# A new order table for a gated-recurrence and MLP kernel on one core: engines, turns and places of some 1,070 steps

## The chip, the cores and the metric

The kernel runs on one core of a Trainium2 chip. A core has five engines with a queue each: TensorE (PE; its weight loads are listed apart as PEld), VectorE (DVE), ScalarE (ACT), GpSimd (POOL) and SyncE (SP, which here only issues DMAs). Each engine works its queue off in order and waits at semaphores for the others. The metric is the device time of one execution in microseconds (us), as the median of several runs.

## The reference

Inputs are q, k, v, a_re, a_im of shape (4, 8, 768, 48): batch, heads, sequence, head size. First a recurrence with a complex decay for each row of the state, then a layer norm and an MLP with a residual:

```python
mag = np.sqrt(a_re * a_re + a_im * a_im)
scale = np.minimum(mag, 0.999) / (mag + 1e-06)
a_re_n, a_im_n = (a_re * scale, a_im * scale)
...
for t in range(S):
    ...
    new_re = ar * S_re - ai * S_im
    new_im = ar * S_im + ai * S_re
    S_re, S_im = (new_re + kv, new_im)       # kv = outer(k_t, v_t)
    y[:, :, t] = q_t @ S_re
...
x = y with heads joined                       # (4, 768, 384)
xn = (x - mu) / np.sqrt(var + 1e-06) * g_ln
out = x + np.maximum(xn @ w_ch1, 0.0) @ w_ch2 # 384 -> 1536 -> 384
```

## The kernel before

**The tiling.** The sequence is cut into chunks of 128 steps. Two chunks are a pair P; three pairs make a batch, so there are 12 pairs (0 to 11) and 24 chunks n (2P and 2P+1). Pair 0 alone is worked on in two halves of the heads (`PARTS`), so its steps have names such as `r.0.0` and `r.0.1`.

**The steps of a pair**, as they are named in the order table:

- *Loads* on SP: `are`, `aim` (L440), `k`, `q`, `vf` (L399). The weights come by two DMAs from POOL's queue: `wl.0` (w1b, L359) and `wl.1` (w2b, L361).
- *Decay.* `ln` and `iv` on ACT (L443, L445: logarithm of a_re and its reciprocal), `r` (L289: a_im/a_re), `r2` (its square, on ACT L453 or by multiplication L289), `u` (ACT L457: log of 1 + r2), `l` and `lc` (DVE L461, L464), `dec` (PE L472: running sums), `e` and `en` (ACT L476: exponentials). `th` (ACT L480: arctangent), `ph` (PE L487, L491: running phase), `car` (the phase carried to the next pair), `sin`, `cos` (ACT L509, L520, L532), with `qt` (PE L516) or `abs` (L526, L528) between them.
- *Products.* `ke`, `qe`: k times en, q times e (two halves m of 384 elements). `ks`, `qs`: these times cosine (a = 0) and sine (a = 1), 768 elements each. All are multiplications at L289 on DVE or POOL. `dps`, `decc`: the decay at the end of the pair.
- *Chunk by chunk.* `kT`, `qT` (PE transposes, L588) with the copies `ksT`, `qsT` out of PSUM (L284 on ACT, L286 on DVE), or the same by one transposing DMA on SP (L593). `am` (PE L611: 8 products of qsT and ksT), `atm` (DVE: times a triangular mask), `gm` and `G` (the state, L635, L639), `y` (PE L661, L664), `x` (its copy), `bn` (DVE L674, L675), `xtr`, `xT` (transposed x).
- *MLP.* `mm1` (PE L715) in three groups, `relu` (ACT L726 or DVE L728), `mm2` (PE L736), `rstd` (L698 to L703), `ot` (on DVE in one step, L750; or `oa` on ACT, L741, and `ot` on POOL, L748), `st` (the store, SP L756). `wp`, `wc` fold the layer norm into w1b before the first `mm1`.

Steps with logarithm and exponential need one table set of ACT, those with arctangent and sine another: `tab.log` and `tab.trig` are the loads (L770). `warm` (L765) are matmuls without use for their result, at the start.

**What sets the order.** Nothing is scheduled by a program: `PLAN` is a table of tokens `name:engine`, and each engine's queue is the table's order of its own tokens. A number after P, A or V is a PSUM bank. `name:G@other` adds a wait: the step starts only when `other` is done ("turns at the shared port"). Data and buffers bring their own semaphore waits; every tile name has a ring of buffers (`RINGS`, 2 to 10).

```python
name, where = token.split(":")
where, _, ops[name].behind = where.partition("@")
...
for op in steps:
    if op.behind:
        tc.add_manual_dep(made[op.name][0], made[op.behind][-1].name, info, ...)
```

Of the kernel before, what the change touches and what calls it, by code (L numbers as in the profile page):

```python
# [44 lines left out]
warm.23:P0 r.0.1:V warm.24:P0 u.0.0:A warm.25:P0 q.0.1:S warm.26:P0 r2.0.1:V warm.27:P0 uth:V u.0.1:A
warm.28:P0 r.1.0:V warm.29:P0 gln:S warm.30:P0 warm.31:P0 warm.32:P0 r2.1.0:V warm.33:P0 warm.34:P0 are.2.0:S
warm.35:P0 warm.36:P0 l.0.0:V warm.37:P0 warm.38:P0 tab.trig.1:A th.0.1:A warm.39:P1 lc.0.0:V th.1.0:A
ph.0.1:P0 k.0.0:S dec.0.0:P1 th.0.0:A car.0.1:V0 l.0.1:V sin.0.1:A0 q.0.0:S ph.0.0:P2 warm.40:P3 warm.41:P3
car.0.0:V2 q.1.1:S wgc:V ph.1.0:P4 lc.0.1:V tab.log.2:A u.1.0:A k.1.1:S wl.0:G@lc.0.1 dec.0.1:P3 car.1.0:V4
qt.0.1:P0 ln.2.0:A vf.0.0:S l.1.0:V warm.42:P6 ident:G warm.43:P6 warm.44:P6 warm.45:P6 e.0.0:A1 warm.46:P6  # L50
warm.47:P6 vf.0.1:S iv.2.0:A warm.48:P6 lc.1.0:V dec.1.0:P6 en.0.1:A3 r.2.0:V k.1.0:S en.0.0:A1 e.1.0:A6
are.3.0:S r2.2.0:V e.0.1:A3 qe.1.0.0:V u.2.0:A dps.0:P1 ke.0.0.0:V qe.0.0.0:V warm.49:P3 warm.50:P3 l.2.0:V
warm.51:P3 warm.52:P3 warm.53:P3 warm.54:P3 warm.55:P3 warm.56:P3 qe.0.1.0:V warm.57:P3 warm.58:P3
tab.trig.3:A sin.0.0:A2 ke.0.1.0:V cos.0.1:A0 qt.0.0:P2 lc.2.0:V sin.1.0:A4 warm.59:P3 qs.0.0.1:V warm.60:P3
ks.0.0.1:V cos.0.0:A2 ks.0.1.0:V qt.1.0:P4 qs.0.1.1:V th.2.0:A ks.0.1.1:V dps.1:P0 ks.0.0.0:V cos.1.0:A4
kT.1:P2 decc.1:V0 qs.0.1.0:V kT.0:P0 qs.0.0.0:V ksT.1:V2 qT.0:P3 qe.1.0.1:G@qs.0.0.0 qT.1:P4 qsT.0:V3 mask:G
aim.3.0:S tab.log.4:A en.1.0:A6 wp.0:P5 decc.0:V1 qs.1.0.1:V qsT.1:A4 dec.2.0:P2 qs.1.0.0:V vf.1.1:S wc.0.0:V5
ke.1.0.1:G@qs.1.0.0 ksT.0:A0 am.1:P6 wc.0.1:V5 qT.3:P4 vf.1.0:S ke.1.0.0:G e.2.0:A2 wc.0.2:V5 am.0:P0
en.2.0:A2 v.0:G q.2.1:S qsT.3:V4 ks.1.0.0:V ln.3.0:A gm.0:P2 q.2.0:S ph.2.0:P4 atm.1:V6 ks.1.0.1:G@ks.1.0.0
G.0:A2 iv.3.0:A k.2.0:S gm.1:P2 qT.2:P3 atm.0:V0 y.1:P6 r.3.0:G k.2.1:S kT.3:P7 G.1:V2 wp.1:P0 qsT.2:V3  # L60
tab.trig.5:A sin.2.0:A4 are.4.0:S y.0:P1 kT.2:P2 ksT.3:V7 x.0:A1 v.1:G qt.2.0:P4 th.3.0:A ksT.2:V2 xtr.0:P7
aim.4.0:S wl.1:G gm.2:P1 wc.1.0:V0 x.1:A6 ph.3.0:P2 G.2:A1 wc.1.1:V0 qe.2.0.0:G cos.2.0:A4 xtr.1:P6 wc.1.2:V0
gm.3:P1 xT.0:A7 qe.2.0.1:G am.3:P4 sin.3.0:A2 xT.1:V6 wp.2:P0 atm.3:V4 qs.2.0.0:G car.3.0:A2 am.2:P6 qt.3.0:P2
atm.2:V6 mm1.0.0.0:P4 cos.3.0:A2 qs.2.0.1:G mm1.0.0.1:P4 G.3:V1 y.3:P2 wc.2.2:V0 relu.0.0:A4 y.2:P1 x.3:V2
pad.ks.2:G mm1.0.1.1:P6 x.2:A1 wc.2.0:V0 ke.2.0.0:G xtr.3:P2 r2.3.0:A mm1.0.1.0:P6 wc.2.1:V0 ke.2.0.1:G
xT.3:A2 xtr.2:P1 qT.5:P3 bn.1:V xT.2:A1 qT.4:P4 ks.2.0.1:G qsT.5:V3 mm1.1.1.1:P0 qsT.4:V4 vf.2.1:S
mm1.1.1.0:P0 bn.0:V tab.log.6:A u.3.0:A mm1.0.2.0:P2 ks.2.0.0:G are.5.0:S relu.0.1:V6 relu.1.1:A0 mm1.0.2.1:P2
mm1.1.0.1:P4 bn.3:V ln.4.0:A vf.2.0:S mm1.1.0.0:P4 k.3.1:S kT.4:P0 relu.1.0:A4 mm1.1.2.0:P6 ksT.4:V0 k.3.0:S
mm1.1.2.1:P6 iv.4.0:A l.3.0:V kT.5:P0 relu.0.2:A2 aim.5.0:S am.4:P4 lc.3.0:V ksT.5:V0 mm2.0.0:P1
r.4.0:G@lc.3.0 relu.1.2:A6 atm.4:V4 mm2.2.0:P0 are.6.0:S ln.5.0:A mm2.0.1:P1 v.2:G r2.4.0:A mm2.2.1:P0 q.3.1:S  # L70
rstd.0:G am.5:P2 iv.5.0:A gm.4:P4 k.4.0:S atm.5:V2 u.4.0:A dec.3.0:P6 y.4:P5 q.3.0:S G.4:A4 l.4.0:V mm2.0.2:P1
x.4:A5 e.3.0:A6 mm2.1.0:P2 vf.3.0:S r.5.0:V en.3.0:A6 xtr.4:P3 y.5:P4 lc.4.0:V vf.4.0:S mm2.2.2:P0 r2.5.0:V
ln.6.0:A ke.3.0.1:V mm2.1.1:P2 q.4.1:S u.5.0:A ke.3.0.0:V dec.4.0:P6 ks.3.0.0:V x.5:A4 k.4.1:S mm2.1.2:P2
ot.0:V1 e.4.0:A6 qe.3.0.0:G@ks.3.0.0 xtr.5:P4 xT.4:V3 mm2.3.0:P1 en.4.0:A6 aim.6.0:S xT.5:V4 qe.3.0.1:G
ot.1:V2 mm2.3.1:P1 iv.6.0:A bn.2:V mm1.2.0.1:P4 st.0:S bn.4:V rstd.1:G mm1.2.0.0:P4 st.1:S qs.3.0.1:V
mm1.2.1.1:P6 qs.3.0.0:V tab.trig.7:A th.5.0:A mm2.3.2:P1 ks.3.0.1:V relu.2.0:A4 ot.2:V0 mm1.2.1.0:P6 l.5.0:V
st.2:S qT.6:P2 th.4.0:A vf.3.1:S qT.7:P0 q.4.0:S qe.4.0.1:G@l.5.0 qsT.6:A2 kT.7:P3 qsT.7:V0 are.8.0:S
ph.4.0:P4 ke.4.0.0:G ksT.7:V3 relu.2.1:A6 are.7.0:S ot.3:V1 kT.6:P0 sin.4.0:A4 mm1.2.2.0:P2 r.6.0:V abs.4.0:A4
am.7:P6 vf.4.1:S ksT.6:V0 ke.4.0.1:G@r.6.0 mm1.2.2.1:P2 car.4.0:A4 atm.7:V6 cos.4.0:A am.6:P0 k.5.0:S
qe.4.0.0:G mm2.5.0:P4 v.3:A atm.6:V0 ph.5.0:P6 q.6.0:S relu.2.2:A2 lc.5.0:V gm.6:P5 q.5.1:S mm2.5.1:P4  # L80
ks.4.0.0:V abs.5.0:A6 G.6:V5 y.6:P0 mm2.4.0:P1 sin.5.0:A6 k.5.1:S r2.6.0:V ks.4.0.1:V dps.3:P2 cos.5.0:A
aim.7.0:S y.7:P3 x.6:V0 qs.4.0.0:G@ks.4.0.1 mm2.4.1:P1 th.6.0:A x.7:V3 xtr.6:P0 bn.7:V xtr.7:P3 decc.3:A2
aim.8.0:S mm2.4.2:P1 xT.6:A0 bn.5:V gm.7:P5 dec.5.0:P6 qs.4.0.1:V rstd.2:G kT.8:P0 G.7:V5 qsT.8:S tab.log.8:A
en.5.0:A6 mm2.5.2:P4 xT.7:V3 v.4:G ksT.8:V0 mm1.3.1.1:P2 e.5.0:A6 ot.5:V4 k.6.0:S ke.5.0.0:G mm1.3.1.0:P2
u.6.0:A st.3:S mm1.3.0.1:P6 relu.3.1:A2 l.6.0:V vf.6.0:S gm.8:P0 mm1.3.0.0:P6 G.8:A0 qe.5.0.1:V q.5.0:S
ln.8.0:A mm1.3.2.0:P4 ot.4:V1 lc.6.0:V mm1.3.2.1:P4 q.7.0:S iv.8.0:A relu.3.0:V6 ke.5.0.1:G@lc.6.0 gm.9:P0
kT.9:P1 relu.3.2:A4 dps.4:P2 bn.6:V ks.5.0.1:G dec.6.0:P6 ln.7.0:A ksT.9:V1 qT.9:P3 ks.5.0.0:V iv.7.0:A
am.8:P4 mm2.6.0:P1 qsT.9:V3 decc.4:A2 ksT.10:S r.7.0:G@ks.5.0.0 en.6.0:A6 mm2.6.1:P1 G.9:V0 e.6.0:A6 atm.8:V4
mm2.7.0:P0 vf.6.1:S am.9:P2 vf.5.1:S qe.5.0.0:G r2.7.0:A mm2.7.1:P0 st.4:S atm.9:V2 st.5:S qe.6.0.0:G y.8:P4
u.7.0:A k.6.1:S kT.11:P5 x.8:V4 y.9:P2 r.8.0:G vf.5.0:S ph.6.0:P6 x.9:V2 bn.8:V q.6.1:S xtr.9:P4 xtr.8:P2  # L90
tab.trig.9:A sin.6.0:A6 mm2.7.2:P0 xT.9:V4 qs.5.0.1:G xT.8:V2 abs.6.0:A6 ksT.11:V5 mm2.6.2:P1 bn.9:V
mm1.4.0.1:P2 cos.6.0:A rstd.3:G qs.5.0.0:V mm1.4.2.1:P4 car.6.0:A6 l.7.0:V qsT.10:S mm1.4.2.0:P4 th.7.0:A
ke.6.0.1:V mm1.4.0.0:P2 v.6:A ot.7:V0 are.9.0:S ke.6.0.0:G@ke.6.0.1 mm1.4.1.0:P6 relu.4.0:A2 relu.4.2:V4
aim.9.0:S mm1.4.1.1:P6 v.5:A q.7.1:S qT.11:P2 lc.7.0:V relu.4.1:V6 ph.7.0:P4 qe.6.0.1:G@lc.7.0 qsT.11:A2
k.7.1:S dps.6:P0 ks.6.0.1:G ot.6:V1 car.7.0:A4 am.10:P6 k.7.0:S decc.6:A0 r2.8.0:A gm.10:P1 atm.10:V6
mm2.8.0:P0 th.8.0:A qs.6.0.0:G mm2.8.1:P0 abs.7.0:V4 sin.7.0:A4 am.11:P2 mm2.9.0:P6 ks.6.0.0:V rstd.4:G
G.10:V1 dec.7.0:P4 ksT.13:S atm.11:V2 qs.6.0.1:G mm2.8.2:P0 tab.log.10:A u.8.0:A y.10:P1 q.8.1:S ot.8:V0
kT.12:P7 st.7:S x.10:A1 l.8.0:V y.11:P2 ln.9.0:A qsT.12:S qT.13:P3 x.11:V2 mm2.9.1:P6 e.7.0:A4 qsT.13:V3
k.8.0:S xtr.11:P0 en.7.0:A4 xtr.10:P1 qe.7.0.0:G mm2.9.2:P6 are.10.0:S xT.10:V1 xT.11:V0 iv.9.0:A am.13:P2
bn.10:V ke.7.0.1:G mm1.5.0.0:P4 vf.7.1:S ksT.12:V7 qe.7.0.1:G mm1.5.0.1:P4 atm.13:V2 mm1.5.1.1:P0 st.6:S  # L100
r.9.0:G tab.trig.11:A cos.7.0:A st.8:S gm.12:P7 relu.5.0:V4 mm1.5.1.0:P0 vf.7.0:S G.12:A7 ph.8.0:P2
relu.5.1:A0 bn.11:V ke.7.0.0:G k.8.1:S am.12:P4 abs.8.0:V2 sin.8.0:A2 gm.13:P7 ks.7.0.0:G k.9.1:S mm1.5.2.1:P0
th.9.0:A atm.12:V4 mm2.11.0:P2 q.8.0:S r2.9.0:A mm1.5.2.0:P0 lc.8.0:V cos.8.0:A y.12:P3 qs.7.0.0:G@lc.8.0
relu.5.2:V0 ph.9.0:P4 x.12:A3 y.13:P3 ot.9:V6 sin.9.0:A4 mm2.10.0:P0 qs.7.0.1:V x.13:A3 mm2.11.1:P2 abs.9.0:V4
# [697 lines left out]
```

## Time and profile before

| | us |
|---|---|
| median of 3 runs | 195.01 |
| lowest, highest | 194.0, 195.34 |
| the profiled execution: first to last instruction (its span; no other time is listed for it) | 193.1 |
| mean granted TensorE clock | 0.986 |

The profile was taken in an execution of its own. Busy times of engines are sums over its span. Matmuls are pipelined, and the ends that the profile gives them are modelled. The costliest groups, with count, busy time and mean time of one:

| group | engine | count | busy us | mean ns |
|---|---|---|---|---|
| mm2, L736 | PE | 288 | 54.5 | 326 |
| mm1, L715 | PE | 432 | 51.3 | 273 |
| atm, L289 | DVE | 24 | 28.9 | 1219 |
| relu, L726 | ACT | 26 | 26.3 | 1020 |
| table loads, L770 | ACT | 17 | 21.8 | 1283 |
| qs, 768 elements, L289 | POOL | 12 | 19.6 | 1641 |
| qe, 384 elements, L289 | POOL | 18 | 16.4 | 917 |
| ks, 768 elements, L289 | POOL | 9 | 14.7 | 1642 |
| ke, 384 elements, L289 | POOL | 16 | 14.5 | 916 |
| qs, ks, 768 elements, L289 | DVE | 23 | 12.7 | 543, 570 |

### The profile page before, as it was taken

Reading aid. Unit: us, or ns where it says so; the run is one execution under the profiler, and the core shown is the slowest. Engines: PE = TensorE matmul, PEld = TensorE weight load, DVE = VectorE, ACT = ScalarE, POOL = GpSimd, SP = SyncE. Lnnn points to the kernel's source line nnn. Section 1 sums busy time; section 2 is a strip of 40 time slices with the busy share of each in tenths; the row PEclk is TensorE's granted clock in tenths of the full one; section 3 lists DMA queues with packets and bytes.
Section 4 is the critical chain, followed back from the end, with each engine's and each line's share of the span. In section 5 each row is a group of like instructions: output and inputs, shape, how many; then the busy total and the mean of one; then the engine's idle time right before and its main releaser. Section 6 shows DMA issues by size and latency. Waiting matters only on the chain.

```text
span 193.1 us, 5126 instructions
## 1 busy us (share of the span) xinstructions
PE 175.3 (91%) x2042; PEld 133.6 (69%) x2042; DVE 151.7 (79%) x276; ACT 159.4 (83%) x222; POOL 104.8 (54%) x123
## 2 busy tenths in 40 slices
PE   5856597999999999999999989999989897999991
...
PEclk9999969999999999999999999999999999999998
...
DMA packets 129992, 37.04 MB, mean 192 GB/s; under 512 B 124976, under 2 KB 129584, under 8 KB 129968
## 3 DMA queue, kind: packets, MB, share of 16 engines
...
q8 instruction: 16, 0.26, 0.6%
...
## 4 chain that ended last, share of the span: by engine, by line
PE 52%; DVE 17%; ACT 12%; DMA 7%; SPq 4%; issue 4%; POOL 2%; DVEq 0%; ACTq 0%
PE banks L736 16%; PE banks L715 15%; PE banks L588 5%; PE banks L611 3%; DMA qsT<-qs 3%; DMA aim<-in_a_im_dram 2%; SPq L593 2%; PE banks L491 2%; ACT L770 2%; DVE l L461 2%; DMA k<-in_k_dram 2%; ACT trig L509 2%; ACT th L480 2%; PE banks L661 2%; PE banks L682 2%
## 5 line engine op out<-in xcount | busy, mean ns | idle before, releaser
L736 PE MATMUL banks<-w2b,h 128*128 128x384 bf16 x288 | 54.5, 326 | 0.7 <-ACT trig L509 0.6
L715 PE MATMUL banks<-xT,w1b 128*128 128x256 bf16 x432 | 51.3, 273 | 0.0
L715 PEld LDWEIGHTS <-w1b 128*128 128x128 bf16 x432 | 41.3, 98 | 6.3 <-DVE xT L286 0.4
L736 PEld LDWEIGHTS <-h 128*128 128x128 bf16 x288 | 26.1, 97 | 14.6 <-issue 1.1
L289 DVE TENSOR_TENSOR atm<-banks,mask 128x1024 bf16<-128x1024 f32 x24 | 28.9, 1219 | 7.4 <-PE banks L611 7.2
L726 ACT ACTIVATE h<-banks 128x1024 bf16<-128x1024 f32 x26 | 26.3, 1020 | 5.4 <-PE banks L715 5.2
L289 POOL TENSOR_TENSOR qe<-q,e 128x384 bf16<-128x384 f32 x18 | 16.4, 917 | 22.8 <-DVE qs L289 8.4
L289 POOL TENSOR_TENSOR qs<-qe,trig 128x768 bf16<-128x768 bf16 x12 | 19.6, 1641 | 7.7 <-DVE ks L289 5.5
L770 ACT ACT_TABLE_LOAD x17 | 21.8, 1283 | 1.1 <-PEq L786 0.8
L289 POOL TENSOR_TENSOR ke<-k,en 128x384 bf16<-128x384 f32 x16 | 14.5, 916 | 9.9 <-DVE l L464 5.6
L289 POOL TENSOR_TENSOR ks<-ke,trig 128x768 bf16<-128x768 bf16 x9 | 14.7, 1642 | 7.7 <-DVE ks L289 6.8
L611 PE MATMUL banks<-qsT,ksT 128*128 128x128 bf16 x192 | 14.6, 219 | 1.7 <-DMA qsT<-qs 1.7
L728 DVE TENSOR_SCALAR h<-banks 128x1024 bf16<-128x1024 f32 x10 | 12.1, 1214 | 4.9 <-PE banks L715 4.9
L748 POOL TENSOR_TENSOR ot<-ot,x 128x384 f32<-128x384 f32 x8 | 7.2, 914 | 15.8 <-ACT ot L741 15.8
L611 PEld LDWEIGHTS <-ksT 128*128 128x128 bf16 x192 | 12.0, 97 | 4.0 <-issue 2.6
L491 PE MATMUL banks<-th,u_th 128*128 128x384 f16 (+1 forms) x52 | 11.9, 313 | 2.5 <-ACT th L480 2.5
L750 DVE SCALAR_TENSOR_TENSOR ot<-banks,rstd,x 128x384 f32<-128x384 f32 x16 | 9.8, 612 | 5.4 <-PE banks L736 3.5
L461 DVE SCALAR_TENSOR_TENSOR l<-r,w 128x768 f16<-128x768 f16 (+1 forms) x13 | 12.0, 926 | 2.0 <-ACT r L457 1.8
L674 DVE BATCH_NORM_STATS2 stats<-x 128x6 f32<-128x384 bf16 x24 | 13.1, 546 | 0.0
L289 POOL TENSOR_TENSOR r<-aim,are 128x768 f16<-128x768 f32 x6 | 10.9, 1817 | 4.1 <-ACT are L445 4.1
L443 ACT ACTIVATE w<-are 128x768 f32<-128x768 f32 (+1 forms) x13 | 10.3, 797 | 2.5 <-DMA are<-in_a_re_dram 2.5
L457 ACT ACTIVATE r<-r,one_b 128x768 f16<-128x768 f16 (+1 forms) x13 | 11.5, 887 | 0.7 <-DVE r L289 0.6
...
## 6 DMA issues: line engine op xcount, KB each, us to landing
...
w1b<-in_moe_w_ch_dram POOLq DMA_DIRECT2D x1, 1152.0 KB, 11.1
w2b<-in_moe_w_ch_dram POOLq DMA_DIRECT2D x1, 1152.0 KB, 12.5
```

The lines of the kernel that those rows point to most:

```text
L289: {"DVE": nc.vector, "POOL": nc.gpsimd}[eng(name)].tensor_tensor(**kw)
L443: add(f"ln.{X}", lambda S_=S_: act(out=S_("w"), in_=S_("are"), func=AF.Ln), needs=[f"are.{X}"], uses=[("are", P), ("w", P)])
L457: add(f"u.{X}", lambda S_=S_: act(out=S_("r2"), in_=S_("r2"), func=AF.Ln, bias=one_b), needs=[f"r2.{X}", "one"], uses=[("r2", P)])
L461: nc.vector.scalar_tensor_tensor(out=S_("l"), in0=S_("r2"), scalar=0.5, in1=S_("w"), op0=ALU.mult, op1=ALU.add)
L491: nc.tensor.matmul(heads(ps[:, c]), lhsT=u_th[:, c, j], rhs=step(T("th", P), j), start=False, stop=(j == R - 1), skip_group_check=True)
L611: nc.tensor.matmul(ps[:, h], lhsT=T("ksT", n)[:, h], rhs=T("qsT", n)[:, h], start=True, stop=True)
L674: nc.vector.bn_stats(out=T("stats", n), in_=T("x", n))
L715: nc.tensor.matmul(ps[:, jj], lhsT=w1b[:, dc, ts(gi * JG + jj, C)], rhs=T("xT", P)[:, dc].rearrange("p c t -> p (c t)"), start=(dc == 0), ...
L726: act(out=dst, in_=src, func=AF.Relu)
L728: nc.vector.tensor_scalar(out=dst, in0=src, scalar1=0.0, scalar2=None, op0=ALU.max)
L736: nc.tensor.matmul(bank(f"o.{n}")[:, 0:DM], lhsT=T("h", P)[:, j, ts(c, C)], rhs=w2b[:, j], start=(j == 0), stop=(j == NJ - 1))
L770: g.add(f"tab.{nm}.{i}", lambda tab=tab: nc.scalar.preload_act_table_set(tab))
```

## The change

The table is replaced as a whole, and the number of warm-up matmuls in the code goes from 61 to 64. The steps, their code and their buffers stay; names, engines, waits and places in the queues change:

- **The start.** `are` comes for pair 0 first (it was pair 1); `th` of pairs 0 and 1 comes ahead of the first logarithms `u`. `wl.0` waits for `l.0.0` (it was `lc.0.1`), `wl.1` for `qt.2.0` (no wait of its own before). Warm-ups 2, 15, 24 and 42 wait for `r.0.1`, `r2.1.0`, `u.0.0` and `l.2.0`; before, 40 ran in one row at the start.
- **Engines.** ACT to DVE or back: `G` (5 and 2), `relu` (8 and 9), `x` (6 and 8), `xT` (4 and 3), `ksT` (2 and 3), `qsT` (3 and 1), `r2` (4 and 2), `abs`, `car`, `decc`. ACT to POOL: `r2` 2, `rstd` 4 (2 come back), `v` 3. DVE to POOL or back: `ke` 6 and 3, `qe` 4 and 3, `ks` 4 and 4, `qs` 1 and 6, `r` 2 and 1, `ot` 5 and 4, `v` 1.
- **Transposes.** `ksT.12` goes from PE and DVE to a DMA; `ksT.20` and `qsT.17` come from DMAs to PE and DVE.
- **Table loads of ACT:** 18 and not 17; `cos.11.0` gets a load of its own behind `e.11.0` and `en.11.0`.
- **Waits in the table** (`@`): 43 and not 23.
- **Order of the matmul groups:** the three parts of `mm2` of a chunk mostly stand together, and so do the two parts of an `mm1` group. At the end `mm2.23` comes ahead of `mm2.22`.

The diff, cut to its first and last lines:

```diff
 PLAN = """
-ue:G are.1.0:S are.0.0:S are.0.1:S aim.0.0:S pad.ks.1:G warm.0:P0 warm.1:P0 aim.0.1:S warm.2:P0 zdec:G
-pad.qs.1:G warm.3:P0 warm.4:P0 aim.1.0:S pad.ks.0:G warm.5:P0 warm.6:P0 warm.7:P0 one:G cmean:G warm.8:P0
-tab.log.0:A ln.1.0:A pad.qs.0:G warm.9:P0 warm.10:P0 aim.2.0:S qrow:G warm.11:P0 ln.0.0:A warm.12:P0 car0.1:G
...
-oa.21:A2 ot.20:V3 mm1.11.2.1:P0 relu.11.1:A6 bn.22:V ot.21:G mm2.22.0:P2 relu.11.2:A0 mm2.23.0:P4 st.21:S
-st.20:S mm2.22.1:P2 rstd.11:A st.19:S mm2.23.1:P4 mm2.23.2:P4 mm2.22.2:P2 ot.23:V4 ot.22:V2 st.23:S st.22:S
+ue:G ident:G pick:G car0.1:G are.0.1:S tab.log.0:A ln.0.1:A iv.0.1:A are.0.0:S qrow:G are.1.0:S aim.0.0:S ln.0.0:A
+iv.0.0:A r.0.0:V aim.0.1:S r.0.1:V cmean:G car0.0:G ln.1.0:A pad.qs.2:G iv.1.0:A r2.0.0:V aim.1.0:S gln:S uth:V
+tab.trig.1:A th.0.0:A warm.0:P0 warm.1:P0 warm.2:P0@r.0.1 warm.3:P0 warm.4:P0 warm.5:P0 warm.6:P0 warm.7:P0 warm.8:P0
+warm.9:P0 warm.10:P0 warm.11:P0 warm.12:P0 ph.0.0:P2 r.1.0:V car.0.0:V2 are.2.0:S th.0.1:A ph.0.1:P0 q.0.1:S r2.1.0:V
+wgc:V one:G th.1.0:A car.0.1:V0 warm.13:P1 warm.14:P1 warm.15:P1@r2.1.0 warm.16:P1 warm.17:P1 warm.18:P1 warm.19:P1
+warm.20:P1 warm.21:P1 ph.1.0:P6 r2.0.1:V sin.0.0:A2 tab.log.2:A u.0.1:A l.0.1:V u.0.0:A k.0.0:S l.0.0:V lc.0.0:V
...
+st.19:S bn.23:V rstd.11:G st.21:S relu.11.2:A0 mm2.23.1:P2 mm2.23.2:P2 oa.23:A2 ot.23:G mm2.22.0:P1 mm2.22.1:P1
+st.23:S mm2.22.2:P1 ot.22:V1 st.22:S
 """
...
-    for i in range(61):
+    for i in range(64):
         g.add(f"warm.{i}", lambda i=i: nc.tensor.matmul(
```

More of the change, by code (lines that the diff above doesn't have):

```diff
@@ L45 @@
[L45 to L104, printed above, removed]
@@ L105 @@
-car.9.0:A4 qsT.15:S xtr.13:P1 xtr.12:P3 ks.7.0.1:V mm2.10.1:P0 xT.12:V3 ksT.15:S mm2.10.2:P0 v.7:V
-tab.log.12:A u.9.0:A xT.13:V1 dec.8.0:P4 G.13:V7 rstd.5:A aim.10.0:S dps.7:P3 l.9.0:V en.8.0:A4 kT.14:P1
-q.9.1:S mm2.11.2:P2 decc.7:V3 qsT.14:S e.8.0:A4 lc.9.0:V ksT.14:V1 mm1.6.1.1:P6 oa.10:A0 bn.12:V gm.14:P3
-ln.10.0:A ot.10:G are.11.0:S mm1.6.1.0:P6 bn.13:V am.15:P4 relu.6.1:A6 qe.8.0.1:V mm1.6.0.1:P0 vf.8.1:S
-atm.15:V4 qe.8.0.0:G@qe.8.0.1 mm1.6.0.0:P0 vf.8.0:S mm1.6.2.1:P6 ke.8.0.1:G ke.8.0.0:V relu.6.0:A0
@@ L115 @@
-mm1.7.1.1:P0 relu.7.0:A4 lc.10.0:V mm1.7.1.0:P0 ot.12:V7 st.11:S ke.9.0.1:G@lc.10.0 r2.11.0:A k.10.0:S bn.15:V
-mm2.14.0:P4 relu.7.1:A0 ke.9.0.0:G relu.7.2:V2 mm2.13.2:P6 vf.9.1:S rstd.7:G gm.16:P5 am.17:P0 ks.9.0.1:V
-q.10.1:S mm2.14.1:P4 ot.13:V6 qe.9.0.0:G@ks.9.0.1 tab.trig.13:A th.10.0:A atm.17:V0 mm2.14.2:P4 q.10.0:S
-dps.9:P2 cos.9.0:A am.16:P6 st.12:S decc.9:V2 ph.10.0:P0 G.16:A5 k.10.1:S atm.16:V6 ks.9.0.0:G th.11.0:A
-mm2.15.0:P5 sin.10.0:A0 car.10.0:V0 y.16:P2 qe.9.0.1:V ksT.19:S y.17:P3 x.16:V2 dec.10.0:P6
```

114 lines of the change are left out of this document (88 added, 26 removed).

## The prediction

> **What bounds the kernel now.** I read the page first, then busy time by stretch, the chain of waits, and the timeline of the start, the end and single operations.
>
> ```profile
> span 193.1 us, 5126 instructions
> PE 175.3 (91%) x2042; PEld 133.6 (69%) x2042; DVE 151.7 (79%) x276; ACT 159.4 (83%) x222; POOL 104.8 (54%) x123
> ...
> PE   5856597999999999999999989999989897999991
> ...
> PEclk9999969999999999999999999999999999999998
> ```
> ```profile
> 0.00:40.00 40.00, 30.22 (x319) 22.31 (x320) 29.79 (x61) 34.69 (x51) 20.00 (x42) 0.96 0.98 211
> 40.00:80.00 40.00, 40.00 (x484) 31.87 (x483) 35.47 (x65) 38.59 (x52) 21.91 (x24) 1.00 1.04 216
> 80.00:160.00 80.00, 77.37 (x942) 58.61 (x941) 70.89 (x125) 71.43 (x98) 49.06 (x44) 1.00 0.96 192
> 160.00:189.00 29.00, 27.75 (x304) 20.78 (x301) 15.03 (x28) 14.71 (x24) 13.83 (x14) 1.00 0.77 144
> ```
> The columns of the second view are the stretch, then busy time of PE, PEld, DVE, ACT, POOL, then clock, DMA share and GB/s. PE is full from 40 us on; ACT is 96% busy from 40 to 80 and 89% after, DVE close behind. Matmuls overlap, so idle time hides small holes. The chain of waits gives the true pace:
>
> ```profile
> 7.07 0.57 DVE r L289
> ...
> 44.62 3.93 PE banks L715 x36
> ...
> 51.20 2.62 PE banks L736 x16
> ...
> 158.75 4.99 DMA qsT<-qs
> ```
> 3.93/36 is 0.109 us for a matmul of L715, 2.62/16 is 0.164 for one of L736. Giving every matmul the spacing its kind has back to back, I get 160.8 us of PE work, 6.6 of it warm-up matmuls. From the first matmul of L715 (below) to the end of the last of L736 (188.85) are 149.1 us: 140.6 of work and 8.5 in which nothing was started (0.5 before 80 us, 6.3 from 80 to 160, 1.6 after). So the run is 39.8 (start) + 140.6 + 8.5 (holes) + 4.3 (last output) = 193.2. The median of the runs is 195.0, so 1.9 us lie around the span. A new table can change the start, the holes and the tail.
>
> ```profile
> 9.55 1.28 ACT L770 ACT_TABLE_LOAD   x1
> 10.85 1.67 ACT L480 ACTIVATE th<-r 128x384 f16<-128x384 f16 x3
> ...
> 39.79 0.28 PE L715 MATMUL banks<-xT,w1b 128*128 128x256 bf16 x1
> ```
>
> **The start, step by step.** Durations are those that the same steps had in before: a half-width step of pair 0 on ACT 0.5 us, a full one 0.8 to 0.95, a table load 1.28; on DVE r 0.55 and 0.95, r2 0.36 and 0.55, l 0.55 and 0.95, lc 0.26 and 0.35. Neighbours on an engine overlap by about 0.1.
>
> The loads change order, but as many bytes stand ahead of aim.0.0 and aim.1.0 as before, so r.0.0 still starts near 7.1 and r.1.0 near 9. aim.2.0 moves behind q.0.1, k.0.0, q.1.1 and q.0.0 on SP's queue: at 0.8 us for each of these it lands near 15 and not at 10; its user r.2.0 runs near 18, so 3 us cover that. On ACT u now comes after th: the trig load starts when iv.1.0 is done (about 8.0), th.0.0 at 9.35, and the three th end at 11.0 (before: 12.5). On PE two warm-ups run at 2.2 us, and the others wait for r.0.1 (8.2 us). Eleven of them at 0.21 us (the spacing of the first ones of before, at half clock) hold ph.0.0 back to 10.5, and it ends near 11.6. Behind it on DVE stand car.0.0 (0.36), r2.1.0 (0.55), wgc (0.68), car.0.1 and r2.0.1 (0.7 together), to 14.0; sin.0.0 and the next load on ACT end at 13.4, so u.0.1 waits 0.6 for r2.0.1, and u.0.1, u.0.0, u.1.0 run from 14.0 to 15.95. u.1.0 ended at 15.24 before: the 1.5 us are gone, and 0.7 more. l.0.0 ends at 15.7 and now releases wl.0, which starts at 15.75 (14.74 before), so w1b lands near 26.8 (25.8).
>
> From there ACT sets the pace: ln.2.0, two en, iv.2.0, three e and u.2.0 to 20.65, the load to 21.95, five sin and cos to 24.6, th.2.0, a load, en.1.0 to 27.5 (26.6 before), ksT.1 and qsT.2 to 29.4, e.2.0, en.2.0, x.0, ln.3.0, iv.3.0 to 32.85. Meanwhile DVE ends the qs of pair 0 near 25.3 and of pair 1 at 26.5, and atm.0 at 30.2; v.0 on POOL ends at 29.3 (31.2 before). So y.0 starts at 30.3, and the 1.35 us for which PE stood still ahead of gm.0 in before go. They come back on ACT: the load to 34.15, sin.2.0 to 34.9, a wait for r.3.0 (on POOL, now behind ks.1.0.0 on DVE, to 35.55), th.3.0, ksT.3, cos.2.0, car.3.0, sin.3.0 to 39.25, and then qt.3.0 on PE. The first matmul of L715 comes at 39.7 against 39.8. What PE has done by then differs by gm.3 alone (0.25).
>
> wl.1 now waits for qt.2.0 and stands behind r.3.0 and v.1: 36.4 against 35.86, 12.5 us to landing as before, so 48.9. Its first user, mm2.1.0, comes 9.25 us of PE work after 39.7: 48.95. That is no margin; I put nothing in the sum and take it up below.
>
> **What changes engine, counts times mean durations.** ACT: squares -4 x 0.84, conversions of v -3 x 0.82, G -3 x 0.47, qsT -2 x 1.01, rstd -2 x 0.50, xT -0.48; against that relu, ksT, abs, oa, decc one each (1.02, 1.02, 0.81, 0.59, 0.31), x +2 x 0.475 and the 18th load 1.28. Together -4.75 us. DVE: qs +5 x 0.54, qsT +3 x 0.68, G +3 x 0.55, squares +2 x 0.55, against relu, abs, r, ke, x, ksT and others: -0.8. POOL: qs -5 x 1.64, half a ks less, and ke +3, qe +1 (0.92 each), v +4 x 0.83, rstd +2 x 1.08, r +1.82, ot +0.91, two squares: about +6.2. No row has a square on POOL: it lies between 0.92 (384 elements) and 1.82 (768 of f32); 1.65, as for qs, is nearest. PE: transposes +8, 0.45 us; three more warm-ups, in waits. SP: 22 transposes and not 23.
>
> By stage, adding the tables at these durations: through the first 40 us of PE work ACT has 62.3 (60.7 before), over the next 80 it has 79.0 (84.5) and DVE 78.4 (83.9). I followed ACT and PE by hand to the first matmul of pair 2 and found them in step: 63.3 us with 2.15 us more PE work done, where before stood at 61.5. So the gain, if any, is after 63 us, where the 6.3 us of holes were. Their larger ones are 0.87, 0.81, 0.40 and 0.31 us on DVE, 0.43 on ACT, 0.75 and 1.27 on DMA transposes. Five us less on each of ACT and DVE, and qs off POOL ahead of the transposes (qs.10.0.1 to am.20: 8.3 us of PE work, was 5.6), should shorten them. But qs.9.0.0 to am.19 shrinks from 6.1 to 4.4, against 4.3 us from issue to landing of a qsT: up to 1 us is lost there. I take 5.4 us of holes, 3 fewer.
>
> The 18th load is in the sum at its row, 1.28; in the quoted rows th starts 0.02 us behind a load. [...]
>
> The tail: cos.11.0 waits for the extra load, but ends some 1.5 us ahead of mm2.19.0, and ksT.22 would land about 2.5 us ahead of am.22. At the end ot.22 follows mm2.22.2 in both: 4.3 us again.
>
> **Sum.** 39.7 + (140.6 + 0.25 + 0.45) + 5.4 + 4.3 = 190.7, plus 1.9 is **192.6**.
>
> **Rivals.** *Holes only move.* 43 instructions have a wait of their own in the table where 23 had (4 of them warm-ups); a new table has its own near misses, and most of before's holes weren't on ACT. 8.5 us again: 193.8 + 1.9 = 195.7.
>
> *GpSimd's reads become the bound (slower).*
> ```profile
> 124.85 1.23 DVE L289 TENSOR_TENSOR ke<-k,en 128x384 bf16<-128x384 f32 x1
> ...
> 124.75 0.91 POOL L289 TENSOR_TENSOR ke<-k,en 128x384 bf16<-128x384 f32 x1
> ```
> This product takes 0.55 us elsewhere on DVE; met by a POOL product it took 1.23 (and l.11.0 1.39, not 0.95). The other DVE products with both inputs in SBUF hardly ever ran beside POOL, so the two take turns. Adding POOL and those DVE operations from the last matmul of L715 of pair 2 to that of pair 9: 80.4 us beside 88.8 of PE work before, 89.6 beside 90.7 after. The room falls from 8.4 to 1.1 us; if half of the 7.3 reaches PE, 195.7 + 3.7 = 199.4. It decides once POOL's products end later than PE's use of them. Against it: POOL names only 2% of the chain, and buffers of two and three give lead. [...]
>
> *The start slips.* Idle PE to 8.2 us, w1b a microsecond later, w2b without margin: 1 to 2.5 us and unchanged holes, 196.7 to 198.2.
>
> **Chances.** Within 1% (1.95 us) is about what a measurement of this kernel can tell from none. Forecast 0.44 (190.2 to 193.0, faster); holes move 0.26 (same); turns 0.20 (slower); start 0.10 (0.02 same, 0.08 slower). The range goes from 3.0 us of holes (190.2) to just short of the middle of the turns case, 199.
>
> **What would show it.** First matmul of L715 at 39 to 40.5; ACT busy near 154.7, POOL near 111; holes after 63 us below 5 us; am.20 without a wait, am.19 with up to 1 us. Wrong if mm2.1.0 waits for w2b, if DVE products stretch to 1.2 us in numbers, or if the chain names POOL above 5%.

## The result, and the profile after

The changed kernel takes 195.20 us, the median of 20 runs (194.16 to 196.86); the kernel before took 194.12 (20 runs, 193.46 to 195.41) beside it. The ratio is 1.0063, with a 95% interval of 1.0044 to 1.0082: about 1.2 us slower, where 192.6 was forecast. A ratio leaves out executions over 1.5% above the fastest of the same kernel, which matters for `e4` below alone: five of its ten, the traced one among them, and with all ten it is 0.999 and not 0.995.

The page of the changed kernel, the same four lines as before:

```profile
span 192.9 us, 5176 instructions
PE 177.0 (92%) x2053; PEld 134.9 (70%) x2053; DVE 153.7 (80%) x276; ACT 155.8 (81%) x214; POOL 113.4 (59%) x134
...
PE   1398399999999999999999999999999999999991
...
PEclk9999958999999999999999999999999999999998
```

Busy time by stretch (columns as before: stretch, then PE, PEld, DVE, ACT, POOL, clock, DMA share, GB/s):

```profile
0.00:40.00 40.00, 28.79 (x274) 19.96 (x274) 28.09 (x55) 30.86 (x43) 18.15 (x40) 0.91 0.98 213
...
80.00:160.00 80.00, 79.71 (x991) 62.05 (x989) 68.33 (x125) 73.91 (x104) 56.94 (x55) 1.00 1.00 203
160.00:189.00 29.00, 29.00 (x324) 22.42 (x320) 19.22 (x33) 14.30 (x21) 12.09 (x16) 1.00 0.62 125
```

Two things happened, and they nearly cancel. From 80 to 160 us PE is busy for 79.7 us and not 77.4, and from 160 to 189 without a pause: most of the holes are gone. But in the first 40 us PE and ACT each do less (28.8 us and not 30.2; 30.9 and not 34.7), and the granted clock there is 0.91 and not 0.96. The kernel starts its main work late.

Put into the terms of the prediction, with the same spacing of matmuls:

| us | before | forecast | after |
|---|---|---|---|
| first matmul of mm1 | 39.8 | 39.7 | 44.2 |
| PE work from there | 140.6 | 141.3 | 141.3 |
| holes | 8.5 | 5.4 | 3.5 |
| tail | 4.3 | 4.3 | 3.9 |
| span | 193.1 | 190.7 | 192.9 |

The two spans differ by -0.2 where the medians differ by +1.1. One execution of each kernel was traced: that of the changed kernel is 0.6 us below the median span of its runs (193.5), and that of before is some 0.7 above the 192.4 that its executions of 194.1 us show in later runs. So the terms tell where time went, and the timed ratios how much.

The chain of waits of the changed kernel, its start (start and length in us, engine, what, line):

```profile
17.21 1.18 DVE l L459
18.44 0.82 PE banks L467 x4
...
22.62 1.19 DVE l L456
23.86 1.46 PE banks L760 x6
...
27.25 2.25 PE banks L760 x10
29.50 3.28 PE banks L583 x48
...
43.81 0.48 PE banks L511 x2
44.29 0.76 PE banks L710 x6
```

(Lines are 5 lower than before: L760 is `warm`, L710 `mm1`, L583 the transposes, L459 `lc`.) Warm-up matmuls, which compute nothing, stand in the chain twice, and one `lc` takes 1.18 us where the row of before says 0.35. The timeline of the same stretch, all engines, shows who stood beside whom:

```profile
17.17 1.00 POOL L350 MEMSET qs<- 128x512 bf16 x2
17.21 1.17 DVE L459 TENSOR_SCALAR l<-l 128x768 f16<-128x768 f16 x1
...
20.06 1.28 POOL L284 TENSOR_TENSOR ke<-k,en 128x384 bf16<-128x384 f32 x1 [1.89 <-DVE r L284]
...
20.48 1.74 DVE L284 TENSOR_TENSOR qe<-q,e 128x384 bf16<-128x384 f32 x2
...
22.62 1.18 DVE L456 SCALAR_TENSOR_TENSOR l<-r,w 128x768 f16<-128x768 f16 x1
...
22.95 1.62 POOL L284 TENSOR_TENSOR ks<-ke,trig 128x384 bf16<-128x384 bf16 x1
...
23.73 1.26 DVE L284 TENSOR_TENSOR qe<-q,e 128x384 bf16<-128x384 f32 x1
...
23.86 1.46 PE L760 MATMUL banks<-u_e 128*128 128x256 f16 x6 [0.84 <-DVE l L456]
...
25.25 0.50 PE L511 MATMUL banks<-qrow,pick 1*128 1x192 f16 x2
...
25.79 0.49 ACT L515 ACTIVATE trig<-banks 128x384 bf16<-128x384 int16 x1 [1.37 <-PE banks L511]
...
27.18 2.31 PE L760 MATMUL banks<-u_e 128*128 128x256 f16 x10
27.29 0.81 ACT L515 ACTIVATE trig<-banks 128x768 bf16<-128x768 int16 x1 [1.01 <-PE banks L511]
```

Each long DVE step lies beside a GpSimd step: `lc.1.0` beside the memsets `pad.qs.0` and `pad.qs.1` (L350), two `qe` (1.74 for both, 1.02 where GpSimd is idle) beside `ke.0.0.0`, `l.2.0` beside `qe.1.0.0`, the third `qe` (1.26 and not 0.55) beside `ks.0.0.1`. In brackets stand the idle time ahead of a step and who ended it: six warm-ups on PE waited for `l.2.0`, `qt.0.1` (L511) stood behind them, and ACT waited for it and for `qt.1.0`.

### The profile page after: what moved, and what is told of

Same layout as the page of the kernel before. It is cut to its first block, busy times and chain, and to the rows that moved or that the text cites. A ratio compares the mean times of both kernels' runs of the same rounds, so it can differ in the third digit from the quotient of the medians.

```text
span 192.9 us, 5176 instructions
## 1 busy us (share of the span) xinstructions
PE 177.0 (92%) x2053; PEld 134.9 (70%) x2053; DVE 153.7 (80%) x276; ACT 155.8 (81%) x214; POOL 113.4 (59%) x134
## 4 chain that ended last, share of the span: by engine, by line
PE 72%; ACT 11%; DVE 8%; POOL 2%; issue 2%; DMA 2%; SPq 1%; DVEq 0%; POOLq 0%; ACTq 0%
PE banks L731 22%; PE banks L710 21%; PE banks L583 5%; PE banks L606 4%; PE banks L760 4%; PE banks L467 3%; ACT h L721 2%; PE banks L486 2%; DMA aim<-in_a_im_dram 2%; PE banks L656 2%; PE banks L677 2%; PE banks L659 2%; DVE l L456 2%; PE banks L634 2%; ACT e L471 1%
## 5 line engine op out<-in xcount | busy, mean ns | idle before, releaser
L731 PE MATMUL banks<-w2b,h 128*128 128x384 bf16 x288 | 53.1, 326 | 0.0
L710 PE MATMUL banks<-xT,w1b 128*128 128x256 bf16 x432 | 51.9, 272 | 0.1
L710 PEld LDWEIGHTS <-w1b 128*128 128x128 bf16 x432 | 40.9, 98 | 6.1 <-issue 0.7
L284 POOL TENSOR_TENSOR ke<-k,en 128x384 bf16<-128x384 f32 x19 | 17.6, 933 | 18.3 <-ACT en L471 6.5
L765 ACT ACT_TABLE_LOAD x18 | 23.1, 1283 | 1.1 <-PEq L781 0.8
L284 POOL TENSOR_TENSOR qe<-q,e 128x384 bf16<-128x384 f32 x19 | 17.4, 924 | 10.5 <-DVE l L459 3.5
L760 PE MATMUL banks<-u_e 128*128 128x256 f16 x64 | 12.9, 356 | 10.2 <-DVE r L284 5.3
L760 PEld LDWEIGHTS <-u_e 128*128 128x128 f16 x64 | 7.3, 122 | 14.6 <-DVE r L284 6.0
L284 POOL TENSOR_TENSOR ks<-ke,trig 128x768 bf16<-128x768 bf16 (+1 forms) x9 | 14.7, 1639 | 3.5 <-DVE qs L284 2.1
L284 POOL TENSOR_TENSOR r<-aim,are 128x768 f16<-128x768 f32 x7 | 12.7, 1814 | 5.5 <-DVE ks L284 2.8
L284 POOL TENSOR_TENSOR qs<-qe,trig 128x768 bf16<-128x768 bf16 x7 | 11.5, 1639 | 6.1 <-DVE qs L284 1.7
L486 PE MATMUL banks<-th,u_th 128*128 128x384 f16 (+1 forms) x52 | 12.7, 332 | 0.0
L723 DVE TENSOR_SCALAR h<-banks 128x1024 bf16<-128x1024 f32 x9 | 11.0, 1217 | 2.0 <-PE banks L710 2.0
L743 POOL TENSOR_TENSOR ot<-ot,x 128x384 f32<-128x384 f32 x9 | 8.2, 911 | 7.1 <-ACT ot L736 6.5
## 6 DMA issues: line engine op xcount, KB each, us to landing
w2b<-in_moe_w_ch_dram POOLq DMA_DIRECT2D x1, 1152.0 KB, 12.7
```

Source lines behind the costliest of these rows:

```text
L284: {"DVE": nc.vector, "POOL": nc.gpsimd}[eng(name)].tensor_tensor(**kw)
L486: nc.tensor.matmul(heads(ps[:, c]), lhsT=u_th[:, c, j], rhs=step(T("th", P), j), start=False, stop=(j == R - 1), skip_group_check=True)
L710: nc.tensor.matmul(ps[:, jj], lhsT=w1b[:, dc, ts(gi * JG + jj, C)], rhs=T("xT", P)[:, dc].rearrange("p c t -> p (c t)"), start=(dc == 0), ...
L723: nc.vector.tensor_scalar(out=dst, in0=src, scalar1=0.0, scalar2=None, op0=ALU.max)
L731: nc.tensor.matmul(bank(f"o.{n}")[:, 0:DM], lhsT=T("h", P)[:, j, ts(c, C)], rhs=w2b[:, j], start=(j == 0), stop=(j == NJ - 1))
L760: g.add(f"warm.{i}", lambda i=i: nc.tensor.matmul(bank(f"warm.{i}")[:, 0:256], lhsT=u_e[:, 0, 0], rhs=u_e[:, 1].rearrange("p j t -> p (j t ...
```

## The experiments

**Theory (A):** the start's loss and the gain of the rest are separate and add up. **Rival:** they hang together: the holes are gone because PE came late and everything ahead of it had more lead.

Each ratio below is to a before timed beside it (medians 194.05 to 194.76 us); the changed kernel was not timed again with them. The diffs show single tokens with a neighbour, not whole lines of the table.

### The two halves swapped

`e1` has the tokens of the old table up to the first `mm1`, then what is left of the new table in its order; `e2` the reverse. A few PSUM banks at the seam differ beside that, and each takes `wl.1` as the old table has it, without a wait of its own. `e1` against the changed kernel, its first and last tokens before the seam:

```diff
-ue:G ident:G pick:G car0.1:G are.0.1:S tab.log.0:A
+ue:G are.1.0:S are.0.0:S are.0.1:S aim.0.0:S pad.ks.1:G
...
-wc.2.0:V2 mm1.0.0.1:P6 wl.1:G@qt.2.0 mm1.0.0.0:P6 y.2:P1 relu.0.1:A4
+wc.2.0:V0 mm1.0.0.1:P6 mm1.0.0.0:P6 y.2:P3 relu.0.1:A4
```

> The start of the table of before (all steps ahead of its first matmul of mm1), then the changed table. Theory A, start and rest are separate: first mm1 near 39.8 us as in before, 3.5 us of holes behind it as in the changed kernel, so 39.8 + 141 + 3.5 + 4 = 188.3 span, ratio to before 0.975 to 0.98. Theory B, the late start of the changed kernel is what lets the other engines run ahead and so shortens its holes: the holes come back to about 8 us, span 192.8, ratio 0.995 to 1.0.

> The start of the changed table, then the table of before. Theory A: first mm1 near 44.2 us, 8.4 us of holes, 44.2 + 140.3 + 8.4 + 4.2 = 197.1 span, ratio 1.02. Theory B: the lead of the other engines fills the holes, about 4 us are left, span 192.7 and ratio 1.00 to 1.005.

Measured: `e1` 191.16 us, ratio 0.9825 (0.9772 to 0.9877); `e2` 200.13, ratio 1.0283 (1.0233 to 1.0334), both beside a before of 194.76 and with 4 runs each. The first `mm1` comes at 39.3 and 45.7 us; holes are 4.6 and 8.1. The stretch from 80 to 160 us, first `e1`, then `e2`:

```profile
80.00:160.00 80.00, 79.69 (x976) 62.38 (x973) 67.62 (x121) 73.67 (x101) 56.40 (x54) 1.00 0.99 202
```
```profile
80.00:160.00 80.00, 77.49 (x939) 58.87 (x936) 70.20 (x122) 73.73 (x101) 52.03 (x48) 1.00 0.99 194
```

PE's 79.7 goes with the rest of the new table, 77.5 with that of the old, whatever the start. The stops of `e2` are those of before at the same steps and of about their size (0.81 ahead of mm2.11, 0.87 ahead of xtr.16, 0.63 ahead of am.19); only that of am.20 fell, from 1.27 to 0.50. So the rival falls, and the ratios add within their intervals (1.0283 and 0.9825 together would give 1.011):

| ratio to before | start of before | start of after |
|---|---|---|
| rest of before | 1 | 1.0283 |
| rest of after | 0.9825 | 1.0063 |

The new start costs 2.4 to 2.8% (4.6 to 5.5 us), the new rest gains 1.8 to 2.2% (3.4 to 4.3 us). `e1` is faster than both kernels. Its largest stops are new ones at the seam: 0.55 and 0.19 us in mm1.0.2, and 0.30 ahead of mm2.1.0. `e2` lies above the 1.02 that was expected: its first `mm1` comes 1.5 us later than in the changed kernel, and its clock is at half from 22.7 to 32.9 us, 3.4 us longer. That the one follows from the other was not tested.

### What in the start costs the time

`e3`: the four warm-ups that wait for a step lose that wait.

```diff
-warm.2:P0@r.0.1
+warm.2:P0
...
-warm.15:P1@r2.1.0
+warm.15:P1
...
-warm.24:P1@u.0.0
+warm.24:P1
...
-warm.42:P1@l.2.0
+warm.42:P1
```

> The changed table, with the four waits of warm-up matmuls taken out. If the tied warm-ups hold qt.0.1 and qt.1.0 back (they started 1.9 and 2.3 us after the sines that they need), cos.1.0 ends 2 to 3 us earlier and the first mm1 comes near 41.5; ratio to before about 0.995. If the slip is DVE's products stretched by GpSimd (lc.1.0, qe.0.0.0, l.2.0, qe.0.1.0, 2.5 us together), the first mm1 moves by 0.5 us at most and the ratio stays near 1.006.

Measured: 194.71, ratio 0.9985 (0.9947 to 1.0022); the first `mm1` came 0.2 us earlier (44.0). Neither expectation held: the start hardly moved, and yet the ratio fell. `qt.0.1` moved only from 25.25 to 24.22, because the warm-ups that are now free still write PSUM bank 1, and wait there for `decc.1` to read it:

```profile
22.42 1.86 PE L760 MATMUL banks<-u_e 128*128 128x256 f16 x8 [1.75 <-DVE dec L281]
24.22 0.49 PE L511 MATMUL banks<-qrow,pick 1*128 1x192 f16 x2
```

The clock was at half from 21.0 to 31.3 us, longer than in the changed kernel (23.8 to 30.6). The timed ratio is 0.8% below that of the changed kernel; the trace does not show by what.

`e4`: three memsets of GpSimd lose their waits and go ahead of `wl.0`, right behind the mask. `e5`: besides that, three products of pair 0 and 1 go to DVE, in the gaps that its queue then has.

```diff
+mask:G pad.qs.0:G pad.qs.1:G pad.ks.0:G
...
-pad.qs.0:G@lc.0.1
...
-pad.qs.1:G@l.1.0
...
-pad.ks.0:G@l.2.0
```

and what `e5` adds:

```diff
+qe.1.0.1:V ke.0.0.0:V
...
+lc.2.0:V qe.1.0.0:V
...
+qs.0.0.1:V ks.0.0.1:V
...
-ke.0.0.0:G@r.2.0
...
-qe.1.0.0:G@qe.0.0.0
...
-ks.0.0.1:G@qe.1.0.1
```

> The changed table, with the three memsets pad.qs.0, pad.qs.1 and pad.ks.0 in the idle time of GpSimd ahead of wl.0. If the memsets stretch lc.1.0 (1.17 us, elsewhere 0.35), it is back at 0.35, dec.1.0 and e.1.0 come 0.6 to 0.8 us earlier and the first mm1 up to 0.8. If lc.1.0 is stretched by the weight DMA that GpSimd issues just before, it stays near 1.17 and nothing moves.

> The changed table with the pads early, and ke.0.0.0, qe.1.0.0 and ks.0.0.1 on DVE and not on GpSimd. If GpSimd's products stretch DVE's (qe.0.0.0 1.27, l.2.0 1.18, qe.0.1.0 1.26 us, where 0.55, 0.95, 0.55 are usual), these are back at the usual size; three products more cost 1.45 us of DVE, so the last qs of pair 0 ends near 26.8 (27.94) and the first mm1 comes near 43.0 (44.2). If the slip isn't DVE's, the first mm1 stays within 0.4 of 44.0.

Measured: `e4` 194.91, ratio 0.9954 (0.9902 to 1.0006); `e5` 193.81, ratio 0.9969 (0.9937 to 1.0001). On DVE, `e4` and then `e5`:

```profile
17.48 0.36 DVE L459 TENSOR_SCALAR l<-l 128x768 f16<-128x768 f16 x1
...
19.94 1.74 DVE L284 TENSOR_TENSOR qe<-q,e 128x384 bf16<-128x384 f32 x2
```
```profile
20.23 1.02 DVE L284 TENSOR_TENSOR qe<-q,e 128x384 bf16<-128x384 f32 x2
...
22.10 0.96 DVE L456 SCALAR_TENSOR_TENSOR l<-r,w 128x768 f16<-128x768 f16 x1
```

Without the memsets beside it `lc.1.0` takes 0.36 us and not 1.17 (in `e5` too), while the products still take turns; without the products, those are short too. In `e4` the first `mm1` comes at 43.8. In `e5` the last `qs` of pair 0 ends at 27.2 and not 27.9 though DVE has three steps more, and the first `mm1` comes at 43.1, 1.1 us earlier than in the changed kernel. Both intervals lie below that of the changed kernel. So GpSimd's neighbourhood is a part of the loss: about a quarter of the 4.5 us by the trace, 0.9% by the ratios.

`e6` leaves out warm-ups 40 to 60. `e7` is `e5` and `e6` together.

```diff
-warm.40:P1 warm.41:P1 warm.42:P1@l.2.0 warm.43:P1
...
-warm.48:P1 warm.49:P1 warm.50:P1
...
-warm.58:P1 warm.59:P1 warm.60:P1
```

> The changed table without warm-ups 40 to 60. If these hold the chain back: qt.0.1 starts near 23.5 (25.25), cos.1.0 ends near 25.6 (28.1), qT.0 starts with the last qs at 28.0 (29.3), and the first mm1 comes 1.3 us earlier or more. If the half clock takes it back (32 transposes at 0.108 us and not 0.056, as the granted clock is 0.5 behind an idle PE), the last of them ends near 32.3 as now and the first mm1 stays within 0.4 us.

> e5 and e6 together. If the slip is DVE's stretched steps first and the warm-ups second, the first mm1 comes at 41.5 to 42.5, holes behind it stay at 3.5 to 4.5, ratio to before 0.99. If neither, 43.5 or later.

Measured: `e6` 194.83, ratio 1.0027 (1.0000 to 1.0054); `e7` 194.07, ratio 1.0007 (0.9980 to 1.0034). ACT gained what the tied warm-ups had cost it: in `e6` `cos.1.0` ended at 26.1 (28.1 in the changed kernel) and `en.1.0` at 29.0 (30.9). And yet the first `mm1` came later, at 45.0. PE's timeline tells why; first that of `e6`, then the same steps in `e10`, a run told of below:

```profile
28.79 1.91 PE L581 MATMUL banks<-ident,ks 128*128 128x128 bf16 x16
30.50 2.77 PE L581 MATMUL banks<-ident,qs 128*128 128x128 bf16 x24
```
```profile
27.05 1.05 PE L584 MATMUL banks<-ident,ks 128*128 128x128 bf16 x16
27.94 1.50 PE L584 MATMUL banks<-ident,qs 128*128 128x128 bf16 x24
```

With no warm-ups PE idles (from 23.65 us on it is busy for 1.26 of 3.41), the clock is at half from 23.6 to 33.9 us, and the same 24 transposes take 2.77 us and not 1.50. In `e7` the clock rises at 31.0 and the first `mm1` comes at 43.0, no earlier than in `e5` and between the two times expected. Its ratio also misses the 0.99 expected: in its trace PE also stops for 1.17 us ahead of mm2.1.0, for w2b to land.

That left a question: are warm-ups good or bad here? `e10` keeps `e5`, takes away the wait of `warm.42`, and fills PE's idle time with 14 more.

```diff
+warm.64:P1 warm.65:P1 warm.66:P1 warm.67:P1 warm.68:P1 warm.69:P1 warm.70:P1 warm.71:P1 dps.1:P1
...
-warm.42:P1@l.2.0
+warm.42:P1
...
+warm.72:P1 warm.73:P1 warm.74:P1 warm.75:P1 warm.76:P1 warm.77:P1 qT.0:P6
```

> The kernel of e5 with the wait of warm-up 42 taken out and 14 more warm-ups in idle time of PE (8 ahead of dps.1, 6 ahead of qT.0). If the granted clock is what takes 2 us from the transposes (48 at 0.108 and not 0.056 us), it stays at 1.0 from about 14 us on, qT.0 starts near 27.3, y.0 near 32 and the first mm1 comes at 41 to 42 (43.1 in e5); ratio about 0.988. If idle PE isn't what halves the clock, it falls to 0.5 near 22 to 25 us as before and the first mm1 stays at 43 or later.

Measured: 193.10, ratio 0.9954 (0.9926 to 0.9982), the first `mm1` at 41.1, as expected; the ratio was expected at 0.988 and misses that. Its line of granted clock has no dip:

```profile
PEclk9999999999999999999999999999999999999999
```

With 35 matmuls more than `e7`, which fill the pauses, PE reaches the transposes at 25.97 and ends them at 29.4; `e7` reached them at 26.26 and ended them at 31.5. So of the 4.5 us of the start `e10` takes 3.1 back in its trace, and 1.1% in the timed ratios (its traced execution is the fastest of its ten). Against `e5` the first `mm1` is 2.0 us earlier, but the ratio falls by 0.15% only and the intervals overlap: what the clock does to the start is shown, that all of it reaches the total is not. The 1.3 us that still divide `e10` from before were not traced to a step.

### What in the rest gains it

`e8` undoes the relief of ACT in `e1`: three conversions `v` (3, 6, 10) and six squares `r2` (3, 4, 7, 8, 9, 11) go to ACT, at the same places in the order (ACT's busy time rises by 6.0 us). `e11` undoes that of GpSimd: five `qs` go back to it.

```diff
-v.3:G@l.5.0
+v.3:A
...
-r2.4.0:V
+r2.4.0:A
...
-r2.9.0:G
+r2.9.0:A
```

and in `e11`, with 6.0.1, 8.0.0, 9.0.0 and 11.0.0 likewise:

```diff
-qs.4.0.0:V
+qs.4.0.0:G
```

> The kernel of e1 (start of before, rest of the changed table) with three v and six squares back on ACT, some 7.5 us more for ACT and as much less for DVE and GpSimd together. If the relief of ACT is what shortens the holes: 7 us of holes or more (4.6 in e1), span 191.8 to 193. If it is the order and the places of the table as a whole: 5.5 us or less, span 190.2 at most.

> The kernel of e1 with qs.4.0.0, qs.6.0.1, qs.8.0.0, qs.9.0.0 and qs.11.0.0 on GpSimd, as in before: 8.2 us more for GpSimd, 2.7 less for DVE. If moving qs to DVE is what removed the stops of PE at am that waited for transposed tiles (0.75 and 1.27 us in before), stops at am come back and the holes are 6.5 us or more. If not, they stay below 5.5.

Measured: `e8` 195.06, ratio 1.0060 (1.0033 to 1.0087); `e11` 194.74, ratio 1.0049 (1.0010 to 1.0087), both against `e1` at 0.9825. Holes grew from 4.6 us to 8.9 and 8.5: either edit alone costs the whole gain. In `e8` the stops are where ACT is now late. Its largest (in brackets the idle time before, and who ended it):

```profile
106.91 0.36 PE L633 MATMUL banks<-v,ks 128*128 128x48 bf16 x8 [1.27 <-ACT v L401]
```

The state matmul waits for a `v` that stands in ACT's queue. In `e11` the stops were expected at the products `am` that wait for transposed tiles; only 0.59 us ahead of am.22 is of that kind. The others are at gm.6 (1.32), kT.17 (0.80), y.10 (0.72) and gm.18 (0.68). GpSimd and DVE of `e11` ahead of gm.6:

```profile
70.58 1.64 POOL L283 TENSOR_TENSOR qs<-qe,trig 128x768 bf16<-128x768 bf16 x1 [1.03 <-issue]
72.18 1.14 POOL L403 TENSOR_SCALAR v<-vf 128x768 bf16<-128x768 f32 x1
74.68 0.91 POOL L283 TENSOR_TENSOR ke<-k,en 128x384 bf16<-128x384 f32 x1 [1.36 <-DVE ke L283]
75.56 0.83 POOL L403 TENSOR_SCALAR v<-vf 128x768 bf16<-128x768 f32 x1
```
```profile
70.72 1.91 DVE L283 TENSOR_TENSOR qs<-qe,trig 128x768 bf16<-128x768 bf16 x1
72.55 0.98 DVE L458 TENSOR_SCALAR l<-l 128x768 f16<-128x768 f16 x1
```

A `qs` on DVE takes 1.91 us beside one on GpSimd (0.55 else), and `lc` 0.98; so the `ke` of DVE is late, GpSimd waits 1.36 us for it, and the `v` behind that ends when gm.6 already waits. Ahead of y.10 and kT.17 two `ks` on DVE took 2.47 and 2.24 us together in the same way, and gm.18 waits for a `v` in GpSimd's queue. This is the turn-taking of the prediction's slower rival, which the new table avoids here by keeping `qs` off GpSimd. `e11` gives the five no wait of their own, where before had one for three of them (`qs.4.0.0:G@ks.4.0.1`, and 8.0.0 and 9.0.0), so what they would cost with turns is open. Both edits keep the order and move nine or five steps, so they show that these steps must be where the new table has them, not that a reordered table could do no better.

### One stop of `e1` removed

The 0.55 us at the seam of `e1` were a wait for `xT` on DVE behind `ke.2.0.1`. `e9` gives that product to GpSimd.

```diff
-ke.2.0.1:V cos.3.0:A2
+cos.3.0:A2
...
-ke.2.0.0:G
+ke.2.0.0:G ke.2.0.1:G
```

> The kernel of e1 with ke.2.0.1 on GpSimd and not on DVE, where it took 1.61 us beside GpSimd's products (0.55 elsewhere) and held the steps wc.2, so that mm1.0.2.1 stopped for 0.19 and 0.55 us. If that stretch is the cause, those two stops go, holes fall from 4.6 to about 3.8 us and the ratio to before from 0.9825 to about 0.979. If the wait comes from elsewhere, the holes stay at 4.6.

Measured: 190.30 (6 runs), ratio 0.9805 (0.9776 to 0.9835): the best version, though not apart from `e1` by these intervals. The two stops in mm1.0.2 are gone, as expected, but the one ahead of mm2.1.0 grew from 0.30 to 0.96 us, so holes are about 4.4 us and not 3.8. Its chain of waits:

```profile
35.51 13.91 DMA w2b<-in_moe_w_ch_dram
49.42 0.04 issue
49.46 2.11 PE banks L730 x12
```

PE now waits for the second weights, the place for which the prediction found no margin. The same stop stands in most traces with an earlier first `mm1` than the changed kernel's: 0.39 us in `e10`, 0.50 in `e3`, 1.17 in `e7`, 1.78 in `e4`, none in `e5`. So it takes back a part of what an earlier start gains. An earlier issue of that load was not tried.

## Why the prediction was wrong

**The step that failed** is the start: "The first matmul of L715 comes at 39.7 against 39.8". It came at 44.2, and `e1` and `e2` show that the new start costs 4.6 to 5.5 us of the total. Everything else together was better than forecast by 2.3 us. The forecast followed each step of the start and was still close at 16 us (`u.1.0` ended at 16.1, forecast 15.95); then three things came in that it had priced at nothing.

1. *DVE beside GpSimd.* The forecast took `lc` at 0.35 and the products at 0.55 from rows where GpSimd is idle: before had no product or memset on GpSimd between 17 and 24 us. Measured, `lc.1.0` cost 0.82 more, the first two `qe` 0.72, `l.2.0` 0.23 and the third `qe` 0.71, together 2.5. The last `qs` of pair 0 ended at 27.9 and not 25.3. `e4` and `e5` show the cause by taking the neighbours away; of the 2.5 us, 1.1 reach the first `mm1`.
2. *Warm-ups in the way.* The prediction priced eleven warm-ups ahead of `ph.0.0` and put down the three that are new as "in waits". One of them waits for `l.2.0`, and what is queued behind it on PE was not followed. `qt.0.1` ran at 25.25 though its sine was there at 23.3; ACT stood still for 1.37 us and then 1.01 us behind it, and `en.1.0` ended at 30.9 and not 27.5. Ten more warm-ups stood ahead of the first transpose, 1.35 us after its data was ready. `e6` shows the first part: without them `en.1.0` ended 2.0 us earlier.
3. *The clock.* The forecast took PE's steps as they were before, with 3.4 us of half clock (24.0 to 27.4); now it was 6.8 us, from 23.8 to 30.6, behind 3.42 us in which PE was busy for 0.88. In it warm-ups stand 0.21 us apart and not 0.11, transposes 0.107 and not 0.056. `e6` lengthens it to 10.2 us, and the first `mm1` comes 0.7 us later; `e10` removes it, and it comes 1.9 us earlier than in `e7`, where nothing waits for warm-ups 40 to 60 either. Half clock alone is not the price: in `e8` and `e11`, with the start of before, it lasts as long (20.3 to 27.2 and 20.6 to 27.5 us; mean granted clock 0.982 and 0.978, and 0.991 in `e1`), and the first `mm1` comes at 39.3 and 39.4, as in `e1` with 3.4 us of it. So in these runs it cost time where PE's own steps set the pace, as the transposes of `e7` did. The eleven early warm-ups were priced at 0.21 us and took that; the view lists a granted clock of 1.00 for that stretch, but warm-ups stand 0.21 us apart up to 6.9 us in before and up to 13.4 in the changed kernel, as they do at 0.50.

**Holes.** The direction was right and the size too small: 3 us fewer forecast, 5.0 measured (`e1` and `e2` confirm that it belongs to the rest of the table). am.20 goes without a wait, as forecast; the loss of up to 1 us at am.19 did not come. `e8` shows that the first reason given, less work on ACT, is needed for it, and `e11` the other, `qs` off GpSimd, though by DVE's and GpSimd's turns and not by the transposed tiles that were named. Since either edit alone costs the whole gain, they don't say how much belongs to each.

**Work, loads and tail.** PE's work was as forecast. Eighteen table loads took 1283 ns each, as the row said. ACT's busy time was 155.8 (forecast 154.7), GpSimd's 113.4 (111). w2b was issued at 40.9 and not 36.4, since all of the start was late, and PE was as late: it cost 0.19 us. The tail lost 0.4.

**The rivals.** *The start slips* was the right case, with the wrong size: 1 to 2.5 us were given to it, 4.5 came, and holes were not unchanged. *Holes only move* is out, though its 195.7 lies nearest to the 195.2 measured: that is luck, a late start and fewer holes that nearly cancel, not its mechanism. *GpSimd's reads become the bound* is out for the stretch it was made for: GpSimd names 2% of the chain, and the sines' and cosines' products on DVE are as short as ever (of its other products two in the start and one at 160 us took over 1.2 us):

```profile
L284 DVE TENSOR_TENSOR qs<-qe,trig 128x768 bf16<-128x768 bf16 x15 | 7.9, 551 | 0.0
...
L284 DVE TENSOR_TENSOR ks<-ke,trig 128x768 bf16<-128x768 bf16 x14 | 7.3, 550 | 0.0
```

But its mechanism, DVE and GpSimd steps that hold each other up, is what hit the start, where one chain of DVE steps sets the pace (2.5 us more on DVE); and `e11` shows that it would cost the long stretch too with five `qs` more on GpSimd and no turns for them (1.0049 and not 0.9825). The prediction weighed it by totals over the long stretch only, and did not see that the steps moved off GpSimd were those that meet DVE's. The memsets it did not think of: `lc.1.0` took 1.17 us beside them and 0.36 in `e4`, where they had gone ahead. The prediction's sum counted on DVE only steps with both inputs in SBUF; `lc` has one and was stretched all the same.
